# Float64 weights converted with one instruction fewer, and softmax row sums spread by a copy and transposes, in a fused attention and two-MLP kernel

## The chip, the cores and the metric

The kernel runs on one core of a Trainium2 chip. The metric is the time of one execution in microseconds of device time; less is better. The engines are named as the profile names them: PE (TensorE, matrix products; PEld is its weight load), DVE (VectorE), ACT (ScalarE), POOL (GpSimd) and SP (SyncE, which here only issues DMAs).

## The reference

Attention over 4 batches of 12 heads, 448 positions and 64 values per head, and then two feed-forward layers over the 1792 tokens of width 768:

```python
def rmsnorm(x, g):
    return x / np.sqrt(np.mean(x * x, axis=-1, keepdims=True) + 1e-06) * g
scores = (1 / np.sqrt(64)) * rmsnorm(q, g_q) @ rmsnorm(k, g_k).T
attn = np.exp(scores - scores.max(-1))
attn = attn / (attn.sum(-1) + 1e-09)
x = attn @ v                                   # then (1792, 768)
x = (sigmoid(x @ w_gate) * (x @ w_val)) @ w_out          # 768 -> 1536 -> 768
out = np.maximum(x @ w_in2, 0) ** 2 @ w_out2             # 768 -> 2048 -> 768
```

q, k, v and the gains are float32. [...]

## The kernel before, in words

The work runs in four sweeps, one for each batch of 448 tokens. A sweep goes through the weights in 68 blocks of 128 x 768 values (24 for gate and value, 12 for the first output, 16 and 16 for the second layer). Between the blocks of sweep s the kernel places, by a list of slots, the attention of batch s + 1, in six pairs of heads. The attention of batch 0 is the prologue, ahead of the first sweep, in an order written out by hand with due times. A scheduler with a time model of its own orders what the program leaves free.

**Weights.** Only the first sweep converts. `w_load` brings a block of float64 words (768 KB) into one of three raw buffers; `w_conv` turns it into float32. Float64 in little-endian order is a low and a high 32-bit word, and the two are read with a stride of two. ACT multiplies the high word, read as a float32, by 2^-112 (L137), which moves the exponent to where the result needs it. DVE masks the sign out of the high word, in place (L140), shifts ACT's result left by three bits and joins the sign (L144), and joins the top three bits of the low word (L146). `w_store` writes the block to DRAM by a DMA issued on POOL's queue (L153), and the later sweeps read that copy (L120). `w_split` then makes a rounded high part on ACT (L164) and the rest on DVE (L165), for products in three matmuls (L510 to L512, L615 to L617). The first 12 blocks are used unsplit (L539). Converted blocks lie in three buffers (`wraw`), the first 12 in the split buffers.

**Attention of batches 0 and 1.** For a pair of heads: squares and norms (`stat_*`, with a power on POOL, L232), transposes of q and k by PE (L244), scores (L262), row maxima on DVE (L268), exponentials with their row sums on ACT (L280), transposes of the probabilities (L295) and copies of them out of PSUM (L304, L305). `s_rec` adds 1e-9 to the 112 x 4 x 2 sums and takes reciprocals on DVE (L287, L288). `pv_mm` multiplies by v (L313) and then makes, from the reciprocals, a 128 x 448 matrix in PSUM that has on each of the 64 rows of a head that head's reciprocal for every query: eight small matmuls, each with one column of reciprocals repeated 64 times as the stationary operand and an identity as the moving one (L318). ACT copies that matrix (`x_rec`, L326), DVE multiplies the product by it (`x_sum`, L331), and ACT and DVE split the result (L335, L339). Batches 2 and 3 have an attention of their own, which the diff doesn't touch.

**Buffers.** The pool `tmp` has four slots of 128 x 512 float32 for everything short-lived: squares (`sq`), the copy `rs`, the gate's `t` and `e`, the second layer's `rl` and `r2`, output tiles. PSUM has four accumulators (`acc`) and two attention tiles (`att`).

Of the kernel before, what the change touches and what calls it, by code (L numbers as in the profile page):

```python
# [8 lines left out]
F32 = mybir.dt.float32  # L9
F32R = mybir.dt.float32r  # L10
I32 = mybir.dt.int32
AF = mybir.ActivationFunctionType
ALU = mybir.AluOpType
# [4 lines left out]
def attention_moe_moe2_kernel(  # L18
# [14 lines left out]
    nc = tc.nc  # L33
    B, H, S, D = q.shape
# [7 lines left out]
    QC = 4  # L42
    QR = S // QC
# [4 lines left out]
    scale = 1.0 / float(D) ** 0.5  # L48
# [5 lines left out]
    tmp_p = ctx.enter_context(tc.tile_pool(name="tmp", bufs=4))  # L54
# [8 lines left out]
    ident = const.tile([128, 128], F32, name="ident")  # L63
# [59 lines left out]
    def w_conv():  # L123
        i = pos["conv"]
        pos["conv"] += 1
        if i >= NB:
            return
        r = raw64.pop(i).rearrange("p (f t) -> p f t", t=2)
        lo, hi = r[:, :, 0], r[:, :, 1]
        if i < NPLAIN:  # L130
            sp = wsp_p.tile([128, 2, 768], F32R, tag="wsp", name="wsp")
            t = sp[:, 0].bitcast(F32)
            wsp[i] = sp
        else:
            t = wraw_p.tile([128, 768], F32, tag="wraw", name="wraw")
        ti = t.bitcast(I32)
        size = nc.scalar.activation(out=t, in_=hi.bitcast(F32), func=AF.Copy, scale=2.0 ** -112)  # L137
        if pinned[0]:
            tc.keep_in_program_order(size)
        sign = nc.vector.tensor_scalar(  # L140
            out=hi, in0=hi, scalar1=-(2 ** 31), scalar2=None, op0=ALU.bitwise_and)
        if pinned[0]:
            tc.keep_in_program_order(sign)
        nc.vector.scalar_tensor_tensor(  # L144
            out=ti, in0=ti, scalar=3, in1=hi, op0=ALU.logical_shift_left, op1=ALU.bitwise_or)
        nc.vector.scalar_tensor_tensor(  # L146
            out=ti, in0=lo, scalar=29, in1=ti, op0=ALU.logical_shift_right, op1=ALU.bitwise_or)
        wraw[i] = t

    def w_store():  # L150
# [17 lines left out]
    def w_ahead(i):  # L168
        while True:
            if pos["split"] <= min(i + 3, pos["conv"] - 1):  # L170
                w_split()
            elif pos["conv"] <= min(i + (3 if pos["conv"] < NPLAIN + 2 else 4), pos["load"] - 1, pos["split"] + 2):
                w_conv()
            elif pos["load"] <= min(i + 8, NALL - 1) and (
                    pos["load"] <= pos["conv"] + 2 if pos["load"] < NB
                    else pos["load"] <= pos["split"] + 2):
                w_load()
            else:
                break
# [105 lines left out]
    def s_rec(st):  # L285
        su = st["su"]
        nc.vector.tensor_scalar(out=su, in0=su, scalar1=1e-9, scalar2=None, op0=ALU.add)  # L287
        nc.vector.reciprocal(out=su, in_=su)  # L288

    def c_mm(st, c, lo, hi):  # L290

        p = st.pop(("p", c)).rearrange("p e s -> p (e s)")
        for j in range(NS):
            ps, kc = (lo, j) if j <= NF else (hi, j - NF - 1)
            nc.tensor.transpose(ps[:, kc, 0:QR], p[:, j * 128:(j + 1) * 128], ident[:QR, :QR])  # L295
        if c == 0:
            st["pt"] = pt_buf(st)
        st["c", c] = lo, hi
# [8 lines left out]
    def pv_mm(st, o, rt):  # L307


        v, pt = st["v"], st.pop("pt")  # L310
        for kc in range(NF + 1):
            for e in range(2):
                nc.tensor.matmul(  # L313
                    out=o[e * D:(e + 1) * D], lhsT=v[:, kc, e], rhs=pt[:, (NF + 1) * e + kc if kc < NF else NF],
                    start=(kc == 0), stop=(kc == NF))
        for c in range(QC):
            for e in range(2):
                nc.tensor.matmul(  # L318
                    out=rt[e * D:(e + 1) * D, c * QR:(c + 1) * QR],
                    lhsT=st["su"][:, c, e:e + 1].to_broadcast([QR, D]), rhs=ident[:QR, :QR],  # L320
                    start=True, stop=True)
        st["o"], st["rt"] = o, rt

    def x_rec(st):
# [313 lines left out]
    def slots_of(b):  # L638
# [5 lines left out]
        def do_s(key, c0):  # L644
            st = pairs[key]
            for c in (c0, c0 + 1):
                s_mm(st, c, att_tile())
            for c in (c0, c0 + 1):
                s_max(st, c)
                mid.append((s_exp, (st, c)))  # L650
            if c0 == 2:
                later(1, s_rec, st)
# [7 lines left out]
        def do_pv(key):  # L660
            st = pairs[key]
            ps = att_tile()
            pv_mm(st, ps[:, 0, :S], ps[:, 1, :S])
            for fn in (x_rec, x_sum, x_hi):
                mid.append((fn, (st,)))
            later(1, x_lo, st)
            later(1, lambda: pairs.pop(key))
# [113 lines left out]
    def prologue():  # L781
# [63 lines left out]
        for hp in range(HP):  # L845
            key = (0, hp)
            rush[0] = (30, 300, 0)[min(hp, 2)]
            for c in range(QC):
                t = 4 * hp + c
                at(t, lambda key=key, c=c: s_mm(pairs[key], c, att_tile()))  # L850
                at(t, lambda key=key, c=c: s_max(pairs[key], c))
                at(t + 0.5, lambda key=key, c=c: s_exp(pairs[key], c))
                at(t + 1.75, lambda key=key, c=c: c_mm(pairs[key], c, acc4(), acc4()))
                at(t + 2.25, lambda key=key, c=c: c_copy(pairs[key], c, (act, dve)))
            at(t + 2.5, lambda key=key: s_rec(pairs[key]))
            at(t + 3, lambda key=key: pv_mm(pairs[key], acc_tile()[:, :S], acc_tile()[:, :S]))
            at(t + 3.75, lambda key=key: x_rec(pairs[key]))
            at(t + 4.25, lambda key=key: x_sum(pairs[key]))
        rush[0] = 0
        for i in range(5):  # L860
            at(6 + 3 * i, w_load)
            if i < 2:
                at(14 + 4 * i, w_conv)
                at(15 + 4 * i, w_split)
# [29 lines left out]
    for r in range(2):  # L894
# [3 lines left out]
        out=gqk, in0=gains[:, 0:1], scalar=scale, in1=gains[:, 1:2], op0=ALU.mult, op1=ALU.mult)  # L898
# [49 lines left out]
```

## Time and profile before

| | |
|---|---|
| median of three runs | 1309.39 us (1307.68 to 1309.93) |
| the profiled execution's own time | 1309.2 us |
| its span, first to last instruction | 1307.1 us |
| PE busy | 1284.9 us, 98% of the span |
| DVE busy | 938.4 us, 72% |
| ACT busy | 781.7 us, 60% |
| POOL busy | 130.3 us, 10% |
| prologue | 0 to 97.6 us |
| first sweep | 97.6 us to about 430 us |

The busy shares are means over stages with different limits. PE's matmuls overlap, so a matmul of 448 columns shows some 0.37 us but the next one starts about 0.2 us later. A float32 matmul that runs in two passes leaves two records. Lines (L137) are those of the kernel above.

### The profile page before, as it was taken

How to read it: one execution, taken by the hardware profiler on the slowest of the kernel's cores; microseconds unless marked ns; L12 is line 12 of the kernel's file. 1: busy time of each engine (PE TensorE's matmuls, PEld its weight loads, DVE VectorE, ACT ScalarE, POOL GpSimd, SP SyncE). 2: the span in 40 equal slices, each digit the busy share in tenths (PEclk: the TensorE clock that was granted, in tenths of full speed). 3: DMA queues.
4: the chain of work that ended last, by engine and by line, in shares of the span. 5: the costliest groups of instructions: out<-in, count | busy, mean ns of one | idle time of the engine just before them, and what ended most of it. 6: DMA issues, size and time to landing. Idle time of an engine off the chain costs nothing.

```text
span 1307.1 us, 19338 instructions
## 1 busy us (share of the span) xinstructions
PE 1284.9 (98%) x6899; PEld 1120.1 (86%) x6899; DVE 938.4 (72%) x1643; ACT 781.7 (60%) x1600; POOL 130.3 (10%) x100
## 2 busy tenths in 40 slices
PE   8999999999899999999999999999999999999998
PEld 6554488788697999999999999999999999999998
DVE  6876999899898678768986478877897544435521
ACT  5764687568666678656664477765676455524421
POOL 3201214210221001000010000100010000000000
PEclk9999999999899999999999999999999999999999
DMA  5426897787788434333343533434324343333331
GB/s 144 103 76 216 273 292 246 252 270 218 245 232 273 130 113 121 105 114 107 107 113 105 146 97 110 125 100 114 99 86 121 116 127 109 109 109 109 108 114 46
DMA packets 155807, 189.62 MB, mean 145 GB/s; under 512 B 76096, under 2 KB 119616, under 8 KB 155712
## 3 DMA queue, kind: packets, MB, share of 16 engines
q1 hardware_dynamic: 148416, 161.19, 43.0%
q0 software_dynamic: 5440, 26.74, 5.0%
q8 instruction: 55, 0.90, 0.3%
q10 hardware_dynamic: 1856, 0.46, 0.2%
q14 instruction: 40, 0.33, 0.1%
HBM read 150.60 MB, written 32.24 MB: 140 GB/s over the span
## 4 chain that ended last, share of the span: by engine, by line
PE 73%; issue 10%; DVE 7%; DMA 4%; ACT 4%; POOL 2%; POOLq 0%; ACTq 0%; SPq 0%; DVEq 0%
PE acc L510 15%; PE acc L511 15%; PE acc L512 15%; PE acc L617 5%; PE acc L615 5%; PE acc L616 5%; PE att L398 3%; PE att L439 2%; DMA w<-wraw 2%; PE att L470 2%; POOL ms L232 1%; DVE nm L268 1%; PE att L472 1%; ACT p L280 1%; PE acc L313 1%
## 5 line engine op out<-in xcount | busy, mean ns | idle before, releaser
L165 DVE TENSOR_TENSOR wsp<-wraw,wsp 128x768 fp32r<-128x768 f32 x260 | 248.0, 954 | 130.8 <-ACT wsp L164 125.9
L510 PE MATMUL acc<-xy,wsp 128*128 128x448 f32 x888 | 326.7, 368 | 0.2 <-ACT rl L592 0.2
L512 PE MATMUL acc<-xy,wsp 128*128 128x448 f32 x888 | 326.1, 368 | 0.0
L511 PE MATMUL acc<-xy,wsp 128*128 128x448 f32 x888 | 325.9, 367 | 0.0
L164 ACT CAST wsp<-wraw 128x768 fp32r<-128x768 f32 x260 | 216.6, 834 | 130.9 <-PE acc L617 64.7
L512 PEld LDWEIGHTS acc<-xy,wsp 128*128 128x128 f32 x888 | 166.9, 188 | 16.1 <-issue 2.7
L510 PEld LDWEIGHTS acc<-xy,wsp 128*128 128x128 f32 x888 | 166.8, 188 | 16.1 <-issue 0.9
L511 PEld LDWEIGHTS acc<-xy,wsp 128*128 128x128 f32 x888 | 166.9, 188 | 15.0 <-issue 1.5
L232 POOL TENSOR_TENSOR ms<-ms,mhalf 112x16 f32<-112x16 f32 (+1 forms) x25 | 91.1, 3648 | 577.1 <-DVE ms L231 486.8
L616 PE MATMUL acc<-wsp,rb 128*128 128x384 f32 x384 | 129.2, 336 | 0.0
L617 PE MATMUL acc<-wsp,rb 128*128 128x384 f32 x384 | 129.0, 336 | 0.0
L615 PE MATMUL acc<-wsp,rb 128*128 128x384 f32 x384 | 128.8, 335 | 0.0
L510 PE MATMUL acc<-hb,wsp 128*128 128x448 f32 x288 | 106.2, 369 | 0.0
L511 PE MATMUL acc<-hb,wsp 128*128 128x448 f32 x288 | 105.5, 367 | 0.0
L512 PE MATMUL acc<-hb,wsp 128*128 128x448 f32 x288 | 105.5, 367 | 0.0
L417 ACT ACTIVATE p<-att,nm,ms 112x448 f32<-112x448 f32 x96 | 68.8, 724 | 34.7 <-DVE nm L408 34.5
L137 ACT ACTIVATE wraw<-raw 128x768 f32<-128x768 f32 x56 | 51.5, 920 | 51.8 <-DMA w<-wraw 27.8
L592 ACT ACTIVATE rl<-acc 128x448 f32<-128x448 f32 x64 | 35.0, 547 | 70.7 <-PE acc L512 69.9
L280 ACT ACTIVATE p<-att,nm 112x448 f32<-112x448 f32 x88 | 55.3, 639 | 33.7 <-DVE nm L268 32.3
L617 PEld LDWEIGHTS acc<-wsp,rb 128*128 128x128 f32 x384 | 72.1, 188 | 1.6 <-issue 1.3
L616 PEld LDWEIGHTS acc<-wsp,rb 128*128 128x128 f32 x384 | 72.1, 188 | 0.8 <-issue 0.7
L615 PEld LDWEIGHTS acc<-wsp,rb 128*128 128x128 f32 x384 | 72.1, 188 | 0.2
(136 smaller groups left out, 2167.7 us busy)
## 6 DMA issues: line engine op xcount, KB each, us to landing
wraw<-w SPq DMA_DIRECT2D x204, 384.0 KB, 3.0
w<-wraw POOLq DMA_DIRECT2D x56, 384.0 KB, 6.0
raw<-in_moe_w_out_dram SPq DMA_DIRECT2D x28, 768.0 KB, 5.4
raw<-in_moe_w_in_dram SPq DMA_DIRECT2D x16, 768.0 KB, 6.6
raw<-in_moe_w_gate_dram SPq DMA_DIRECT2D x12, 768.0 KB, 6.8
raw<-in_moe_w_val_dram SPq DMA_DIRECT2D x12, 768.0 KB, 6.1
out_dram<-ob SPq DMA_DIRECT2D x28, 192.0 KB, 2.9
qs<-qs SPq DMA_DIRECT2D x24, 224.0 KB, 3.0
```

What stands on the lines that cost most here:

```text
L137: size = nc.scalar.activation(out=t, in_=hi.bitcast(F32), func=AF.Copy, scale=2.0 ** -112)
L164: nc.scalar.copy(out=sp[:, 0], in_=t)
L165: nc.vector.tensor_tensor(out=sp[:, 1], in0=t, in1=sp[:, 0].bitcast(F32), op=ALU.subtract)
L232: nc.gpsimd.tensor_tensor(out=ms, in0=ms, in1=mhalf[:QR, 0:ms.shape[1]], op=ALU.pow)
L280: nc.scalar.activation(out=p[:, e], in_=ps[:QR, e, :S], func=AF.Exp, bias=nm[:, e:e + 1], scale=st["rq"][:, c, e:e + 1] if "rq" in st else ...
L417: nc.scalar.activation(out=p[:, i * (S + TAIL):i * (S + TAIL) + S], in_=ps[:QR, i, :S], func=AF.Exp, bias=nm[:, i:i + 1], scale=rq[:, 2 * ...
L510: nc.tensor.matmul(out=o, lhsT=wh, rhs=xh, start=start, stop=False)
L511: nc.tensor.matmul(out=o, lhsT=wh, rhs=xl, start=False, stop=False)
L512: nc.tensor.matmul(out=o, lhsT=wl, rhs=xh, start=False, stop=stop)
L615: nc.tensor.matmul(out=o, lhsT=rh, rhs=wh, start=(k1 == 0), stop=False)
L616: nc.tensor.matmul(out=o, lhsT=rh, rhs=wl, start=False, stop=False)
L617: nc.tensor.matmul(out=o, lhsT=rl, rhs=wh, start=False, stop=(k1 == K2 - 1))
```

## The change

In the conversion, ACT's instruction becomes a parametric ReLU with the same scale and a slope of 2^32 for negative inputs. A negative value so gets an exponent that is larger by 32, and the shift by three bits carries that bit into the sign's place. The mask of the sign falls away. In its place DVE shifts the low word right by 29 bits and writes the result over the high word; the instruction that shifts ACT's result joins that. The third DVE instruction is gone.

In the attention of batches 0 and 1, `s_rec` has a third instruction: POOL copies the eight reciprocals of each query, each repeated 64 times, to a tile of 112 x 512 from the `tmp` pool. `pv_mm` transposes the four 112 x 128 parts of that tile in place of the eight matmuls.

```diff
-        size = nc.scalar.activation(out=t, in_=hi.bitcast(F32), func=AF.Copy, scale=2.0 ** -112)
+        size = nc.scalar.activation(
+            out=t, in_=hi.bitcast(F32), func=AF.Prelu, scale=2.0 ** -112, alpha=2.0 ** 32)
...
-        sign = nc.vector.tensor_scalar(
-            out=hi, in0=hi, scalar1=-(2 ** 31), scalar2=None, op0=ALU.bitwise_and)
+        low3 = nc.vector.tensor_scalar(
+            out=hi, in0=lo, scalar1=29, scalar2=None, op0=ALU.logical_shift_right)
...
         nc.vector.scalar_tensor_tensor(
             out=ti, in0=ti, scalar=3, in1=hi, op0=ALU.logical_shift_left, op1=ALU.bitwise_or)
-        nc.vector.scalar_tensor_tensor(
-            out=ti, in0=lo, scalar=29, in1=ti, op0=ALU.logical_shift_right, op1=ALU.bitwise_or)
...
         nc.vector.reciprocal(out=su, in_=su)
+        sb = st["sb"] = tmp_p.tile([128, 512], F32, tag="tmp", name="sb")[:QR].rearrange(
+            "p (c e d) -> p c e d", c=QC, e=2)
+        nc.gpsimd.tensor_copy(out=sb, in_=su.unsqueeze(3).to_broadcast([QR, QC, 2, D]))
...
+        sb = st.pop("sb")
         for c in range(QC):
-            for e in range(2):
-                nc.tensor.matmul(
-                    out=rt[e * D:(e + 1) * D, c * QR:(c + 1) * QR],
-                    lhsT=st["su"][:, c, e:e + 1].to_broadcast([QR, D]), rhs=ident[:QR, :QR],
-                    start=True, stop=True)
+            nc.tensor.transpose(
+                rt[:, c * QR:(c + 1) * QR], sb[:, c].rearrange("p e d -> p (e d)"), ident[:QR, :QR])
```

## Rows read from the trace of the kernel before

**Rows 1.** Busy time by stretch: us, busy (instructions) per engine, clock, DMA.

```profile
0.00:97.60 97.60, 90.34 (x594) 53.84 (x594) 70.66 (x127) 63.00 (x155) 20.70 (x18) 1.00 0.43 107
97.60:170.00 72.40, 67.78 (x229) 37.56 (x229) 57.05 (x84) 42.61 (x82) 14.86 (x17) 1.00 0.77 250
170.00:425.00 255.00, 247.99 (x1380) 205.89 (x1380) 231.63 (x343) 173.82 (x343) 53.79 (x55) 0.99 0.81 252
425.00:1307.10 882.10, 878.83 (x4706) 822.77 (x4700) 579.04 (x1090) 502.23 (x1021) 40.96 (x11) 1.00 0.37 110
```

**Rows 2.** Groups by line and shape: count | busy us, mean ns | idle before.

```profile
L146 DVE SCALAR_TENSOR_TENSOR wraw<-raw,wraw 128x768 int32<-128x768 int32 x56 | 53.3, 952 | 0.2
L137 ACT ACTIVATE wraw<-raw 128x768 f32<-128x768 f32 x56 | 51.5, 920 | 51.8 <-DMA w<-wraw 27.8 <-DVE wsp L165 15.0 <-issue 2.5
L140 DVE TENSOR_SCALAR raw<-raw 128x768 int32<-128x768 int32 x68 | 38.1, 560 | 14.5 <-ACT wraw L137 10.4 <-ACT wsp L137 3.6
L146 DVE SCALAR_TENSOR_TENSOR wsp<-raw,wsp 128x768 int32<-128x768 int32 x12 | 11.5, 958 | 0.2
```

**Rows 3.** Chain of waits, one pair of the prologue: start us, us, what.

```profile
55.88 0.38 PE acc L244 x4
56.26 3.16 PE acc L313 x16
59.42 0.79 PE acc L318 x16
...
60.23 0.54 ACT rs L326
...
62.68 1.01 DVE nm L268
```

**Rows 4.** PE's waits from 97.6 to 170 us: total us, times, longest.

```profile
PE att L244 <- ACT p L280: 2.0, 1, 2.0
...
PE acc L539 <- DVE wsp L146: 0.9, 1, 0.9
```

**Rows 5.** PE's waits from 170 to 414 us.

```profile
PE att L313 <- ACT pt L304: 3.4, 1, 3.4
```

**Rows 6.** Timeline round that wait: start us, us, instruction [idle before].

```profile
323.90 0.95 DVE L144 SCALAR_TENSOR_TENSOR wraw<-wraw,raw 128x768 int32<-128x768 int32 x1
...
328.30 1.82 DVE L146 SCALAR_TENSOR_TENSOR wraw<-raw,wraw 128x768 int32<-128x768 int32 x2
...
337.48 0.89 ACT L137 ACTIVATE wraw<-raw 128x768 f32<-128x768 f32 x1 [3.57 <-DMA w<-wraw]
```

**Rows 7.** Chain of waits right behind it.

```profile
341.60 6.12 PE att L313 x16
347.72 0.86 PE att L318 x15
```

**Rows 8.** Busy time in the ten microseconds from 340, columns as in rows 1.

```profile
340.00:350.00 10.00, 8.15 (x41) 5.66 (x42) 7.95 (x11) 5.04 (x10) 1.08 (x2) 0.66 0.71 225
```

**Rows 9.** POOL's groups by shape, columns as in rows 2.

```profile
masks.py:197 POOL MEMSET ident<- 128x128 f32 x1 | 0.2, 205 | 0.0
L883 POOL MEMSET mhalf<- 128x16 f32 x1 | 0.1, 112 | 0.3 <-POOLq L932 0.3
```

**Rows 10.** The power on POOL: duration ns min/median/max, first and last start.

```profile
L232 POOL TENSOR_TENSOR ms<-ms,mhalf x25: 1656/2926/7648, 8.3 to 968.6; 112x16 f32<-112x16 f32 x23, 112x8 f32<-112x8 f32 x2
```

**Rows 11.** Timeline, reciprocals of two pairs and the matmuls after the first.

```profile
90.70 0.20 DVE L288 RECIPROCAL su<-su 112x8 f32<-112x8 f32 x1
...
93.35 0.31 PE L318 MATMUL acc<-ident,su 112*64 112x112 f32 x1
...
321.76 0.20 DVE L288 RECIPROCAL su<-su 112x8 f32<-112x8 f32 x1
```

**Rows 12.** ACT's table loads, columns as in rows 2.

```profile
L884 ACT ACT_TABLE_LOAD x1 | 1.3, 1283 | 1.2 <-PEq L932 1.2
```

**Rows 13.** Transposes of q and k on PE, columns as in rows 2.

```profile
L244 PE MATMUL att<-ident,qk 112*128 112x112 f32 x144 | 18.0, 260 | 2.5 <-ACT p L280 2.5
```

More of the change, by code (lines that the diff above doesn't have):

```diff
@@ L136, in w_conv @@
         ti = t.bitcast(I32)
-        size = nc.scalar.activation(out=t, in_=hi.bitcast(F32), func=AF.Copy, scale=2.0 ** -112)
+        size = nc.scalar.activation(
+            out=t, in_=hi.bitcast(F32), func=AF.Prelu, scale=2.0 ** -112, alpha=2.0 ** 32)
         if pinned[0]:
             tc.keep_in_program_order(size)
-        sign = nc.vector.tensor_scalar(
-            out=hi, in0=hi, scalar1=-(2 ** 31), scalar2=None, op0=ALU.bitwise_and)
+        low3 = nc.vector.tensor_scalar(
+            out=hi, in0=lo, scalar1=29, scalar2=None, op0=ALU.logical_shift_right)
         if pinned[0]:
-            tc.keep_in_program_order(sign)
+            tc.keep_in_program_order(low3)
         nc.vector.scalar_tensor_tensor(
             out=ti, in0=ti, scalar=3, in1=hi, op0=ALU.logical_shift_left, op1=ALU.bitwise_or)
-        nc.vector.scalar_tensor_tensor(
-            out=ti, in0=lo, scalar=29, in1=ti, op0=ALU.logical_shift_right, op1=ALU.bitwise_or)
         wraw[i] = t
```

## The prediction

> **What bounds the kernel now.** I read the busy times by stretch first [rows 1]. The reader is to see that TensorE (PE) is the engine with hardly a hole anywhere. After 425 us it is idle for 882.1 - 878.8 = 3.3 us in all, and the two things that the change edits no longer run there: every conversion and every pair of batches 0 and 1 lies ahead of 425 us. So only the first 425 us can move. In them PE is idle for 97.6 - 90.3 = 7.3 us in the prologue, 72.4 - 67.8 = 4.6 us from 97.6 to 170 and 255.0 - 248.0 = 7.0 us from 170 to 425. VectorE (DVE) is busy for 57.1 + 231.6 = 288.7 of the 327.4 us after the prologue, 88%: it is the second bound, felt only where PE runs out of work. That sets the limits at once. Work taken from DVE can give back at most PE's holes; work taken from PE counts in full where PE doesn't wait.
>
> Second come the groups by shape, for the conversion [rows 2]; third the chain of waits through one pair of the prologue [rows 3], where the eight small matmuls for the row sums stand between the big P·V matmuls and the ScalarE (ACT) copy on which DVE's next maximum depends; fourth PE's own waits after the prologue [rows 4, 5] and, round the longest of them, the timeline [rows 6], the chain [rows 7] and the granted clock [rows 8]. The last two questions are whether GpSimd (POOL) has room for its copy [rows 9 to 11] what a table load costs [rows 12], and how long one transpose takes by itself [rows 13].
>
> **The change part by part.**
>
> *Third conversion instruction (L146), removed.* It is 56 x 0.952 + 12 x 0.958 = 64.8 us of DVE [rows 2]. Four of the 68 lie in the prologue, so the stretch after it loses 64 x 0.953 = 61 us and DVE falls from 288.7 to 228 of 327 us (70%). The value is complete one instruction earlier, so the raw buffer, the store by POOL and the split all start at least 0.95 us earlier.
>
> *First DVE instruction (L140).* A mask in place becomes a shift from the low words into the high words: same operation form, width and strides, 0.56 us before and, I take, after. Bounds: 0.56, and 0.95 as the two-input instruction of the same width, which would give back 68 x 0.39 = 27 us of DVE and still leave a relief of 38. Its wait doesn't change: writing the high words must follow ACT's read of them in both kernels. What stands behind it on DVE is the same as before.
>
> *Copy becomes Prelu on ACT (L137).* Same tile, same 0.92 us [rows 2]. The condition, the loaded table, is a rival below.
>
> *Row sums.* Eight matmuls per pair took 0.79 us on the chain [rows 3]; four transposes of the same 112 columns took 0.38 us there (L244). Twelve pairs: 12 x (0.79 - 0.38) = 4.9 us of PE. Six are in the prologue, on the very chain L318, L326, L331, L335, L339, L268 [rows 3], so they count there although PE also waits; six are in the first sweep, where PE is busy 97% of the time. Bounds: 0 if each lands in front of a wait of PE, 4.9 if none does; I take 4.9.
>
> The page "TensorE: Matmul & The Clock Gate" of the Trainium skill (Part 4, PE-mode transpose) speaks against this part: a transpose costs some 275 ns in a kernel, its access latency being most of it. By that four in a row would be 1.1 us, and the sum for the twelve pairs +3.7 us instead of -4.9. The rows show 0.38 us for four, because only the last one's latency is seen; the measured rows decide.
>
> *The copy on POOL.* 112 x 512 elements. No row has it. From below, two memsets (16 and 128 wide: 0.112 and 0.205 us) give 0.83 ns per element, so 0.11 + 496 x 0.00083 = 0.5 us [rows 9]; from above, the slowest elementwise instruction on POOL, the power, has a median of 2.9 us and reaches 7.6 us where DVE is dense [rows 10]. A plain copy is nearer to the memset: I take 1 us, 3 us in the dense stage. It needs the reciprocal (L288) and must end before the transposes. The shortest cover is that of the sixth prologue pair, 90.9 to 93.35 = 2.4 us; in the first sweep one example is 321.96 to 347.7, some 25 us [rows 7, 11]. So I cost it at nothing; without that cover it would be 1 us a pair, 12 us. It adds a wait on POOL: behind it in POOL's queue stand the stores of converted weights and the power of the next pair's norms. A late store keeps one of three weight buffers, and ACT's next conversion stands waiting for it with the exponentials behind.
>
> *Where the relief of DVE lands.* The longest wait of PE after the prologue is 3.4 us, for ACT's copy L304 [rows 5]. ACT came late because its conversion at 337.48 had waited 3.57 us for a store's landing; that store's value had its second instruction at 323.90 and its third only at 328.30, since DVE put other work between [rows 6]. Without the third the store goes out some 3 us or more earlier, which is the whole wait. Behind the gap the granted clock was 0.66 in that ten-microsecond window [rows 8], between the levels 1.2 and 2.4 GHz, and the sixteen P·V matmul records took 6.12 us [rows 7] against 3.16 at full clock [rows 3]: another 3.0 us. A direct wait for L146 adds 0.9 us [rows 4]. Together 0.9 + 3.4 + 3.0 = 7.3 us. Bounds: 0, if the order that the scheduler now draws up puts as many new holes in as it fills; and 4.6 + 7.0 + 3.0 = 14.6 us if PE never waits after the prologue. 7.3 happens to be the middle, and it is what rows trace to the removed instruction.
>
> **Sum.** The profiled execution took 1309.2 us, its span 1307.1 and 2.1 around it; the median of the three runs is 1309.39, so the two can be treated as one. 1309.2 - 4.9 - 7.3 = **1297.0 us**.
>
> **Rivals.**
>
> *A, the forecast:* 1297, own range 1291 to 1302.
>
> *B, the relief finds nothing:* ACT's waits for stores and loads stay, since a store's landing takes several microseconds with or without L146, and the reordered program has its own holes. Only PE's 4.9 us remain: 1304.3, between 1302 and 1308. For it: the waits for exponentials (2.0 us, [rows 4]) don't name the conversion. Against: DVE at 88%.
>
> *C, every hole closes:* 1309.2 - 4.9 - 14.6 = 1289.7, and down to 1284 if the prologue's 7.3 us shrink too.
>
> *D, the other side: the broadcast tile holds a temporary buffer.* It takes one of four slots that the gate, the squares, the ReLU tiles and the rest share, for some 25 us per pair of the first sweep. With three left, an ACT instruction that evicts an accumulator waits for a slot, the accumulators fill up and PE stops. Price per such stop: as the one seen, 3.4 + 3.0 = 6.4 us. One stop more than now cancels the gain on PE (1309.2 - 4.9 + 6.4 = 1310.7); from there on it decides; three give 1323.5. Against it: the one long wait traced above goes back to weight buffers, not to temporary ones [rows 6]; for it: the slots are already full in the gate's stage, where two tiles live over two blocks each.
>
> *E, a second activation table.* If Prelu isn't with Exp and Tanh in the loaded table, conversions between exponentials cost a load before and one after, 1.283 us each [rows 12]: up to 64 x 2 x 1.283 = 164 us of ACT after the prologue, whose 216.4 busy us there [rows 1] become 381 of 327: 53 us late, about 1362. For it: nothing; Relu, Abs, Tanh, Exp, Square and Copy all run under the one load at the start. "ScalarE: Activation LUTs" (Table sets) agrees in so far as it calls the cheap functions filler of every set; it doesn't list Prelu there.
>
> *F, transposes that don't overlap.* Each takes 0.260 us by itself [rows 13]; four end to end are 1.04 us and the twelve pairs cost 12 x (1.04 - 0.79) = +3.0 us. With the relief of A that is 1304.9. Against it: the chain's row of 0.38 us for four. The page on TensorE named above would have it so.
>
> **How the numbers follow.** A 0.45, B 0.22, C 0.13, D 0.14, E 0.03, F 0.03. The time is A's, 1297. What a measurement here can tell from no change is 0.2%, 2.6 us, so faster means under 1306.8 and slower above 1312.0. A and C are faster (0.58), B mostly (0.19 of 0.22), F by a third (0.01): 0.78. The same: 0.03 of B, 0.02 of F, 0.03 of D: 0.08. Slower: 0.11 of D and E: 0.14. The range runs from 1286, which leaves out the lower end of C (0.05), to 1309, which takes in B and leaves out D and E (0.15).
>
> **What would show it.** After: L146 gone, DVE near 228 us between the prologue's end and the end of the first sweep's stretch; L137 still near 920 ns and one table load; the four transposes under 0.45 us in the chain; POOL's copy near 1 us, ended before them; PE's idle time after the prologue some 4 to 7 us in place of 11.6, with no window of low clock; the prologue's end at about 95 us. Wrong would make it: a PE wait for ACT longer than 3 us at a new place with a low clock behind it (D or B), more than one table load (E), an L137 or a shift that grew, or POOL's stores standing behind the copy while ACT waits for their landing.

## The result, and the profile after

| | before | after |
|---|---|---|
| median (range) | 1308.54 us (1307.24 to 1309.93, 4 runs) | 1293.08 us (1291.59 to 1296.15, 4 runs) |
| ratio, 95% interval | | 0.9885 (0.9863 to 0.9907) |
| profiled execution, its span | 1309.2, 1307.1 us | 1292.45, 1290.7 us |

The change takes 15.5 us off; the forecast was 1297.0. Line numbers from here on are those of each run's own kernel, up to a few lines off those of before: the row maximum, L268 there, is L267 in after, the exponentials are L279, the transposes of q and k L243. First the busy times of the page of after, to set beside the table of before:

```profile
PE 1277.4 (99%) x6755; PEld 1113.2 (86%) x6755; DVE 887.2 (69%) x1575; ACT 783.8 (61%) x1600; POOL 127.1 (10%) x112
```

Busy time by stretch of after, cut at the prologue's end, at a point of the first sweep and at the start of the second sweep; it answers to [rows 1]:

```profile
0.00:92.40 92.40, 88.17 (x522) 50.26 (x522) 66.60 (x123) 63.07 (x155) 25.13 (x24) 1.00 0.47 121
92.40:163.00 70.60, 68.10 (x234) 38.67 (x233) 48.64 (x74) 42.95 (x81) 15.04 (x19) 1.00 0.84 279
163.00:416.20 253.20, 249.95 (x1352) 208.91 (x1351) 196.21 (x293) 179.54 (x351) 46.18 (x59) 0.99 0.79 250
416.20:1290.70 874.50, 871.19 (x4653) 815.35 (x4651) 575.75 (x1086) 498.28 (x1015) 40.72 (x11) 1.00 0.38 109
```

The second sweep began at 432.6 us in before and at 416.2 in after, and from there both take 874.5 us (1307.1 - 432.6, and the last row). So all 16.4 us of the span lie ahead of it: 5.2 in the prologue (97.6 to 92.4), 11.2 in the first sweep (335.0 to 323.8). In the prologue PE has 2.2 us less to do (90.34 to 88.17) and is idle for 4.2 us in place of 7.3. In the first sweep it is idle for 5.7 us (70.60 - 68.10 + 253.20 - 249.95) in place of 11.6, and its busy time is 5.3 us shorter, 318.05 us against 323.37 over the whole stretch of before.

Groups by shape in after (count | busy us, mean ns | idle before), which answer to [rows 2, 12, 13]:

```profile
L145 DVE SCALAR_TENSOR_TENSOR wraw<-wraw,raw 128x768 int32<-128x768 int32 x56 | 53.5, 955 | 1.1
L137 ACT ACTIVATE wraw<-raw 128x768 f32<-128x768 f32 x56 | 51.1, 912 | 33.5 <-DVE wsp L164 24.9 <-DMA raw<-in_moe_w_gate_dram 3.8 <-DMA raw<-in_moe_w_val_dram 2.8
L141 DVE TENSOR_SCALAR raw<-raw 128x768 int32<-128x768 int32 x68 | 38.2, 564 | 27.2 <-ACT wraw L137 19.9 <-ACT wsp L137 6.8
L290 POOL COPY sb<-su 112x512 f32<-112x512 f32 x12 | 7.4, 613 | 36.0 <-DVE su L287 21.2 <-ACT p L279 5.3 <-ACT sq L221 5.0
L320 PE MATMUL acc<-ident,sb 112*128 112x112 f32 x24 | 3.6, 273 | 0.0
L884 ACT ACT_TABLE_LOAD x1 | 1.3, 1283 | 1.2 <-PEq L932 1.2
```

The shift over the high word costs what the mask cost (0.56 us), the parametric ReLU what the copy cost (912 ns against 920), and there is still one table load. The wait of L137 for a store's landing, 27.8 us in before [rows 2], is no longer among the first three.

One pair in the chain of waits of after, which answers to [rows 3, 7]:

```profile
187.20 3.16 PE att L315 x16
190.36 0.53 PE att L320 x4
```

The chain of before has one more row of four transposes of q and k, ahead of those in [rows 3]:

```profile
53.58 0.53 PE acc L244 x4
```

From start to start, in the timelines of a prologue pair, the next matmul came 0.87 us after the first of the eight small matmuls in before, and comes 0.44 us after the first of the four transposes in after:

```profile
59.25 0.94 PE L318 MATMUL acc<-ident,su 112*64 112x112 f32 x16
60.12 0.89 PE L295 MATMUL acc<-ident,p 112*128 112x112 f32 x7
```

```profile
68.55 0.60 PE L320 MATMUL acc<-ident,sb 112*128 112x112 f32 x4
68.99 0.55 PE L297 MATMUL acc<-ident,p 112*128 112x112 f32 x4
```

And PE's waits of after from 163 to 416.2 us (total, times, longest), which answer to [rows 5]:

```profile
PE att L243 <- ACT p L279: 2.8, 1, 2.8
PE acc L510 <- ACT rl L592: 0.4, 1, 0.4
```

One wait of 2.8 us is left where before had one of 3.4, at another place. The timeline round it (start us, us, instruction, idle before), and the window of ten microseconds that it falls in with the one behind it:

```profile
382.19 1.01 PE L261 MATMUL att<-kq 64*112 64x448 f32 x4
...
384.52 0.57 DVE L141 TENSOR_SCALAR raw<-raw 128x768 int32<-128x768 int32 x1 [1.34 <-ACT wraw L137]
...
385.12 0.96 DVE L145 SCALAR_TENSOR_TENSOR wraw<-wraw,raw 128x768 int32<-128x768 int32 x1
...
386.00 1.08 DVE L267 TENSOR_REDUCE nm<-att 112x2 f32<-112x896 f32 x1
...
387.12 0.63 ACT L279 ACTIVATE p<-att,nm 112x448 f32<-112x448 f32 x1 [2.63 <-DVE nm L267]
...
388.51 1.00 PE L243 MATMUL att<-ident,qk 112*128 112x112 f32 x8 [2.85 <-ACT p L279]
```

```profile
380.00:390.00 10.00, 7.15 (x46) 5.99 (x45) 6.05 (x9) 6.25 (x17) 1.69 (x3) 0.97 0.31 107
390.00:400.00 10.00, 10.00 (x52) 8.67 (x52) 5.41 (x7) 6.73 (x11) 0.00 (x0) 0.86 0.63 179
```

This is how the conversion has a part in a hole, a stretch of idle time, on PE. The scores (L261) are done at 383.20, but the row maximum stands on DVE behind a shift and a join, and the shift waits for ACT's conversion, so that DVE is idle for 1.34 us with the maximum still to do; the exponentials wait for the maximum, PE waits for the exponentials. What counts here is the place in DVE's order, not that DVE is full. In and behind the hole the clock is below full: an estimate of (0.03 + 0.14) x 10 = 1.7 us of PE lost here, against (1 - 0.66) x 10 = 3.4 us in before [rows 8].

### The profile page after: what moved, and what is told of

It is laid out like the page before. It is cut to its first block, busy times and chain, and to the rows that moved or that the text cites. A ratio compares the mean times of both kernels' runs of the same rounds, so it can differ in the third digit from the quotient of the medians.

```text
span 1290.7 us, 19003 instructions
## 1 busy us (share of the span) xinstructions
PE 1277.4 (99%) x6755; PEld 1113.2 (86%) x6755; DVE 887.2 (69%) x1575; ACT 783.8 (61%) x1600; POOL 127.1 (10%) x112
## 4 chain that ended last, share of the span: by engine, by line
PE 86%; DMA 2%; DVE 2%; ACT 1%; issue 1%; SPq 0%; DVEq 0%; ACTq 0%
PE acc L511 19%; PE acc L510 19%; PE acc L512 18%; PE acc L616 6%; PE acc L615 6%; PE acc L617 6%; PE att L398 3%; PE att L439 2%; PE att L470 2%; PE att L315 1%; DMA raw<-in_moe_w_gate_dram 1%; PE att L261 1%; PE att L472 1%; PE att L243 1%; PE att L297 1%
## 5 line engine op out<-in xcount | busy, mean ns | idle before, releaser
L510 PEld LDWEIGHTS acc<-xy,wsp 128*128 128x128 f32 x888 | 166.9, 188 | 16.7 <-issue 2.0
L512 PEld LDWEIGHTS acc<-xy,wsp 128*128 128x128 f32 x888 | 166.9, 188 | 14.1 <-issue 0.7
L231 POOL TENSOR_TENSOR ms<-ms,mhalf 112x16 f32<-112x16 f32 (+1 forms) x25 | 81.8, 3275 | 560.3 <-DVE ms L230 469.8
L137 ACT ACTIVATE wraw<-raw 128x768 f32<-128x768 f32 x56 | 51.1, 912 | 33.5 <-DVE wsp L164 24.9
L279 ACT ACTIVATE p<-att,nm 112x448 f32<-112x448 f32 x88 | 55.2, 635 | 19.8 <-DVE nm L267 17.3
```

The costliest lines, as they stand in the source:

```text
L231: nc.gpsimd.tensor_tensor(out=ms, in0=ms, in1=mhalf[:QR, 0:ms.shape[1]], op=ALU.pow)
L279: nc.scalar.activation(out=p[:, e], in_=ps[:QR, e, :S], func=AF.Exp, bias=nm[:, e:e + 1], scale=st["rq"][:, c, e:e + 1] if "rq" in st else ...
L510: nc.tensor.matmul(out=o, lhsT=wh, rhs=xh, start=start, stop=False)
L512: nc.tensor.matmul(out=o, lhsT=wl, rhs=xh, start=False, stop=stop)
```

## The experiments

All kernels were timed against the kernel before on the same chip (its median was 1308.4 to 1309.0). Prologue, first sweep, PE's idle time, DVE's busy time and ACT's waits in the first sweep are from windows and waits of each profiled run. "ACT for DMA" is the sum of ACT's waits ahead of a conversion for a load or a store of a weight block.

| run | median, us | ratio (95%) | prologue | first sweep | PE idle in it | DVE busy in it | ACT for DMA |
|---|---|---|---|---|---|---|---|
| before | 1308.54 | | 97.6 | 335.0 | 11.6 | 291.8 | 41.6 |
| after | 1293.08 | 0.9885 (0.9863 to 0.9907) | 92.4 | 323.8 | 5.7 | 244.9 | 16.8 |
| conv_only | 1296.13 | 0.9905 (0.9892 to 0.9919) | 97.7 | 321.5 | 2.7 | 243.1 | 16.0 |
| sums_only | 1308.29 | 0.9992 (0.9982 to 1.0002) | 93.0 | 338.8 | 14.5 | 293.9 | 42.6 |
| sums_vs | 1305.41 | 0.9983 (0.9968 to 0.9997) | 92.4 | 336.7 | 12.3 | 293.2 | 46.7 |
| third_off_value | 1315.12 | 1.0041 (1.0027 to 1.0055) | 92.6 | 344.3 | 16.7 | 294.4 | 42.3 |
| conv_third_off | 1313.59 | 1.0038 (1.0024 to 1.0052) | 97.9 | 339.6 | 14.1 | 293.4 | 52.6 |
| conv_dve_load | 1324.76 | 1.0129 (1.0108 to 1.0150) | 126.8 | 321.1 | 2.3 | 244.1 | 21.1 |
| two_slots | 1289.46 | 0.9851 (0.9835 to 0.9868) | 91.9 | 318.4 | 2.3 | 244.7 | 14.3 |
| sb_vs | 1288.19 | 0.9836 (0.9820 to 0.9852) | 94.7 | 318.5 | 2.0 | 244.1 | 22.1 |
| sb_vs_late | 1286.85 | 0.9836 (0.9821 to 0.9852) | 92.0 | 317.9 | 1.3 | 244.2 | 20.9 |
| sb_late | 1286.29 | 0.9829 (0.9815 to 0.9844) | 91.3 | 319.3 | 3.2 | 245.0 | 26.5 |
| copy_func | 1291.93 | 0.9880 (0.9856 to 0.9903) | 91.6 | 322.7 | 4.8 | 244.9 | 15.9 |
| lean | 1285.04 | 0.9828 (0.9806 to 0.9849) | 92.5 | 316.2 | 0.4 | 191.0 | 9.9 |

**The two parts by themselves.** conv_only is the kernel before with the conversion's half of the diff, sums_only with the row sums' half.

> The conversion part alone; the row sums stay as eight small matmuls. Whole change measured: 1308.5 to 1293.1 us, 15.5 us. Theory A (my prediction's terms add up): the matmuls are worth 4.9 us, so the conversion alone gives the other 10.6: about 1298 us (1296 to 1300), with ACT's waits for the landing of stores gone from the 27.8 us that they took in the kernel before, and 64 us less DVE time. Rival 1 (the row sums did more than their matmuls, since the prologue became 5.2 us shorter and not 2.4): the conversion is worth 7 to 8 us, about 1301. Rival 2 (the time comes from the order that the scheduler happens to draw up, and the parts don't add): anywhere from 1293 to 1308, with PE's waits at other places than in the whole change.

> The row sums part alone; the conversion keeps its three DVE instructions. Theory A: PE's work falls by 4.9 us and nothing else, about 1303.6 us (1302 to 1305), and ACT's waits for stores stay near 28 us. Rival 1: the prologue alone becomes 5 us shorter, as in the whole change, about 1300.8. Rival 3 (the tile of 112 x 512 takes a temporary slot for some 25 us a pair and DVE is still dense): a new wait of PE of 3 us or more with a low clock behind it, 1308 or more. Rival 2: 1298 to 1311.

The conversion alone is worth 12.4 us, all of it in the first sweep. Prologue and first sweep of conv_only:

```profile
0.00:97.70 97.70, 90.41 (x593) 53.11 (x593) 66.93 (x123) 63.03 (x155) 20.98 (x18) 1.00 0.45 113
97.70:419.20 321.50, 318.77 (x1656) 249.03 (x1656) 243.07 (x366) 220.91 (x430) 59.39 (x71) 1.00 0.81 259
```

The profiled first sweep is 13.5 us shorter than that of before: PE's idle time falls by 8.9 us, the 3.4 us of low clock go, and 1.2 us are not assigned. The clock's part differs from execution to execution: five of before on the same chip had a mean granted clock of 0.999 and took 1307.4 to 1308.1 us, still some 10 us more than any of conv_only (1295.2 to 1297.7).

The order on DVE that goes with the hole of after stands in conv_only too, and no hole is there. Its timeline, and the window of ten microseconds round it:

```profile
392.85 0.59 DVE L141 TENSOR_SCALAR raw<-raw 128x768 int32<-128x768 int32 x1 [1.32 <-ACT wraw L137]
...
394.36 1.08 DVE L267 TENSOR_REDUCE nm<-att 112x2 f32<-112x896 f32 x1
...
397.25 0.93 PE L243 MATMUL att<-ident,qk 112*128 112x112 f32 x8
```

```profile
390.00:400.00 10.00, 10.00 (x68) 9.40 (x65) 6.28 (x9) 6.35 (x14) 1.05 (x2) 1.00 0.49 163
```

Here PE has 3.5 us of the second layer's matmuls to do, from 393.70 on, before the transposes that waited for the exponentials in after, and is busy for all ten microseconds. Of these two late maxima only the one makes a hole for which PE's own order leaves nothing to do in the meantime.

The row sums alone shorten the prologue by 4.6 us and lengthen the first sweep by 3.8, so the median hardly moves. In that sweep PE is idle for 2.9 us more than in before, and the low clock costs some 6.9 us in place of 3.4. One of the holes in sums_only's timeline, and the two windows there:

```profile
393.62 0.95 DVE L165 TENSOR_TENSOR wsp<-wraw,wsp 128x768 fp32r<-128x768 f32 x1
394.49 0.95 DVE L146 SCALAR_TENSOR_TENSOR wraw<-raw,wraw 128x768 int32<-128x768 int32 x1
...
395.35 1.08 DVE L268 TENSOR_REDUCE nm<-att 112x2 f32<-112x896 f32 x1
...
396.47 0.64 ACT L280 ACTIVATE p<-att,nm 112x448 f32<-112x448 f32 x1 [1.55 <-DVE nm L268]
...
397.87 0.89 PE L298 MATMUL att<-ident,p 112*128 112x112 f32 x7 [2.09 <-ACT p L280]
```

```profile
390.00:400.00 10.00, 6.11 (x33) 4.02 (x29) 9.96 (x14) 6.73 (x14) 1.10 (x2) 0.96 1.02 325
400.00:410.00 10.00, 7.79 (x31) 7.45 (x32) 4.88 (x9) 5.63 (x14) 2.26 (x3) 0.53 0.81 266
```

DVE is busy for 9.96 of 10 us, the maximum stands behind a split and the third instruction, and behind the hole the clock is 0.53. Here DVE is full.

**Is it the earlier value, and with it the store?** My sum traced the gain to the store that starts earlier. These two runs keep that, and give DVE a third instruction back that writes words nobody reads, once on the whole change, once on conv_only.

```diff
+        nc.vector.scalar_tensor_tensor(
+            out=hi, in0=lo, scalar=29, in1=ti, op0=ALU.logical_shift_right, op1=ALU.bitwise_or)
         wraw[i] = t
```

> The whole change, and a third DVE instruction of the same form and width again in each conversion, but off the value's path: it writes to the high words of the raw buffer, which nobody reads, so DVE loses its 65 us of relief while the store and the split can start as early as in the whole change. Theory L (the DVE load decides): 10 us are lost again, 1302 to 1304, DVE above 88% after the prologue. Theory V (the value that is ready one instruction earlier decides, DVE's load does not): stays at 1293 to 1296, with ACT's waits for the landing of stores still near 0. Between the two, 1296 to 1302, both count.

> The conversion part alone (1296.1), and a third DVE instruction off the value's path again; row sums as eight matmuls, so no slot is held. Theory L (DVE's load decides): the whole gain of the conversion is lost, 1306 to 1310. Theory V (the earlier value decides): 1296 to 1299. The run with the whole change and this instruction came to 1315 us, but its tile held a slot.

Both are slower than the kernel before, although ACT no longer waits for a single store. The group of L137 in conv_third_off says what it waits for instead, and the timeline what that does to PE:

```profile
L137 ACT ACTIVATE wraw<-raw 128x768 f32<-128x768 f32 x56 | 51.1, 913 | 56.8 <-DMA raw<-in_moe_w_out_dram 30.9 <-DVE wsp L166 11.1 <-DMA raw<-in_moe_w_gate_dram 6.6
```

```profile
202.21 0.89 ACT L137 ACTIVATE wraw<-raw 128x768 f32<-128x768 f32 x1 [1.25 <-DMA raw<-in_moe_w_out_dram]
203.00 0.52 ACT L305 COPY pt<-att 128x448 f32<-128x448 f32 x1
...
203.57 2.87 PE L314 MATMUL att<-pt,v 128*64 128x448 f32 x9 [2.06 <-ACT pt L305]
```

The third instruction reads the raw buffer, so the next load into it must wait for it; the queue that issues the loads shows this (total us, times, longest):

```profile
SPq L116 <- DVE raw L147: 214.0, 51, 13.0
```

ACT's conversion waits for that load, and the copy of probabilities behind it comes late for PE. The waits for stores have become waits for loads, of the same size (42 to 53 us with three DVE instructions a block whatever they do, 10 to 27 with two or one). So the instruction itself is the cause of the gain, and the earlier value is not enough. The two runs do not tell DVE's load from the longer holding of the raw buffer.

**Load by itself.** conv_dve_load should have told DVE's load from the holding of buffers: conv_only with one more instruction a block, on a tile of its own.

```diff
+    idle = [one.tile([128, 1024], F32, tag="vs", name="idle")[:, :768].bitcast(I32)]
+    nc.gpsimd.memset(idle[0], 0)
...
+        nc.vector.scalar_tensor_tensor(
+            out=idle[0], in0=idle[0], scalar=3, in1=idle[0], op0=ALU.logical_shift_left, op1=ALU.bitwise_or)
```

> The conversion alone, as in the run that took 1296 us, with one more DVE instruction for each of the 68 blocks: a shift and join of 128x768 integers that reads and writes a tile of its own that nothing else uses before the third batch. DVE so has as many instructions per block as in the kernel before, but no raw buffer and no converted buffer is held a moment longer than in the run of 1296 us. If it is DVE's load in itself that opens PE's gaps in the first sweep, the time is that of the kernel before or of the run with a third instruction off the value: 1306 to 1314 us, with two or more waits of PE of 2 us and more and a stretch at a lower granted clock behind each. If it is the time for which the raw buffers are held (the loads of float64 then come late), the time stays within 2 us of 1296.

It missed both expectations. The windows of the added instruction's line alone, then of all of the first stretch:

```profile
0.00:126.80 126.80, 63.27 (x67) 0.87 0.33 84
126.80:200.00 73.20, 1.33 (x2) 1.00 0.84 283
```

```profile
0.00:126.80 126.80, 103.27 (x594) 59.85 (x594) 123.67 (x190) 64.18 (x155) 28.52 (x19) 0.87 0.33 84
```

Since nothing ties the instructions to their blocks, the scheduler put all but one or two of the 68 into the prologue. There 63.3 us of DVE cost 29.1 us, with DVE busy for 98% and the clock at 0.87; the first sweep is that of conv_only. It prices DVE in the prologue and leaves the question for the first sweep open.

**The slot, rival D.** In sb_late the copy to the broadcast tile is issued at the start of `pv_mm`, ahead of the product with v; in sb_vs and sb_vs_late the tile lies in memory idle until the third batch, so no slot is held (sb_vs_late also issues the copy as sb_late does); two_slots holds two slots a pair, each filled by a copy of half the size. sums_vs is sums_only without the slot.

```diff
-        sb = st["sb"] = tmp_p.tile([128, 512], F32, tag="tmp", name="sb")[:QR].rearrange(
+        sb = st["sb"] = one.tile([128, 512], F32, tag="vs", name="sb")[:QR].rearrange(
```

> The whole change with POOL's copy issued at the start of the product with v instead of right behind the reciprocals, so that the tile holds its temporary slot for a few us instead of some 25. Theory of rival D in the prediction (the held slot costs something): 1 to 4 us faster, 1289 to 1292, and POOL's copy ends only shortly before the transposes. Theory A (the slot costs nothing): the same, 1293 within 1.5, or 1 to 2 us slower where the copy (0.61 us) now ends after the eight matmuls of 3.16 us and PE waits for it.

> The whole change with the broadcast tile in memory that lies idle until batch 2 (the tile of the split v), so that it takes no temporary slot; the copy is issued where the change issues it. Theory D (the held slot costs the first sweep time): 4 to 7 us faster than the change's 1293, 1286 to 1289, the stage from the prologue's end to the second sweep near 319 us in place of 323.8, no low clock. Theory A (the slot costs nothing; what the later copy gained, 1286.3, is the luck of another order): 1290 to 1296.

> As the run before (no temporary slot), and the copy is issued at the start of the product with v. The two differ in order alone. Theory D: both the same within 2 us, 1285 to 1289. Rival 2 (luck of the order): they differ by 3 us or more, as the change and its late copy did (1293.1 and 1286.3) although their slots were held for 158 and 132 us in the first sweep, which are not far apart.

> The whole change with two broadcast tiles in two temporary slots, each half filled by a POOL copy and read by two of the four transposes: PE's work is the same, two of four slots are held. Theory D: slower than the change by more than its single slot cost, 1300 or more, with waits of PE for ACT's evictions or exponentials. Theory A: 1290 to 1296.

> The row sums part alone, with the old conversion of three DVE instructions, but with the broadcast tile in memory that lies idle, so that no slot of the pool of short-lived tiles is held. The same part with the slot took 1308.3 us, no less than before. If the held slot ate its gain, this one shows it: 1301 to 1304 us (the prologue 4 to 5 us shorter, the first sweep no longer than before). If DVE's load in the first sweep eats it, through gaps that fall wherever the order of the work lets them, this one also takes 1304 to 1312 us, with PE idle for 8 us and more in the first sweep and at least one stretch at a lower clock.

A held slot is not what costs. Holding two is not slower than holding one (1289.46 against 1293.08; the ranges are apart, the intervals of the ratios just touch), and within 1.3 to 2.6 us of holding none (ranges overlap). What the four have in common is that the hole at 385 us of after is gone and no window of their profiled first sweeps has a low clock: PE is idle there for 1.3 to 3.2 us in place of 5.7. Their edits change the order that the scheduler draws up, and the hole goes with the order: copy_func below, which keeps the order of after, has it again, with a wait of 3.1 us at the same transposes. sb_late does not test the slot's holding time, which came out hardly shorter (132 against 158 us over the first sweep's pairs). Without the slot the row sums alone take 1305.41: the prologue's 5.2 us, and a first sweep still 1.7 longer than in before.

**The ReLU's price, and more relief.** copy_func is the change with the plain copy on ACT; it leaves out the sign of the weights. lean is sb_vs_late with one shift on DVE per block; it leaves out the three lowest bits of the weights.

```diff
-            out=t, in_=hi.bitcast(F32), func=AF.Prelu, scale=2.0 ** -112, alpha=2.0 ** 32)
+            out=t, in_=hi.bitcast(F32), func=AF.Copy, scale=2.0 ** -112)
```

> The whole change, but ACT's instruction is the plain copy with a scale, as in the kernel before, so that the sign of the weights is left out; every engine's instructions stand in the same order. It prices the parametric ReLU. If it costs no more than the copy (before showed 920 ns for the copy, after 912 ns for the ReLU) the time is that of the changed kernel, 1292 to 1295 us, with L137 within 20 ns and one table load. If ReLU with a slope cost something outside of its own record, the time would fall by over 2 us.

> The fastest order of the changed kernel (1286.3 to 1286.9 us: broadcast tile in idle memory, the copy on POOL placed ahead of the transposes), with the low word left out of the conversion: DVE has one shift for each block (some 0.5 us) in place of a shift and a join (some 1.5 us), so the three lowest bits of the weights are missing. If the relief is used up once PE's gaps in the first sweep are closed (1.3 us of idle PE were left), this brings nothing: 1284 to 1288 us. If time goes on falling with DVE's load as it did from three instructions to two (13 us for 0.9 us less per block), it would take 1275 us or less.

The intervals of the change and of copy_func lie all but on each other, so the ReLU has no price that shows. lean has 53 us of DVE less than sb_vs_late in the first sweep, and its median is 1.8 us lower, with intervals that overlap. First sweep of lean:

```profile
92.50:408.70 316.20, 315.80 (x1583) 246.14 (x1583) 191.01 (x302) 222.14 (x430) 60.23 (x77) 1.00 0.80 261
```

PE is idle for 0.4 of 316.2 us there. So the relief saturates: from three DVE instructions to two it is worth 12.4 us (conv_only); from two to one, in an order that had only 1.3 us of holes left, it is worth some 2 us, which is not clear of the noise.

## Why the prediction came out, point by point

- **Bound.** Right. After the start of the second sweep nothing moved (874.5 us in both), and the gain is PE's holes, the clock behind them and PE's work.
- **Removed instruction, as a size on DVE.** Too large. I took 64 x 0.953 = 61 us off DVE and forecast 228 up to 425 us, which is 230.8 for the whole first sweep; it is 244.9, a fall of 46.9 (48.7 in conv_only, where POOL's copy is absent). The 61 us are right as a sum of records: all of DVE's records in the sweep add up to 322.4 us in before and 263.3 in after. But records of neighbours overlap, as the two in 1.82 us of [rows 6] show, by 30.7 us in before and 18.5 in after, so an instruction out of a dense row frees less than its record.
- **Where the relief lands.** The direction held, the size was off: the term was 7.3 us, conv_only shows 12.4, under my upper bound of 14.6. The named step fell. I let one late store stand for the cause; third_off_value and conv_third_off keep the early store and lose the whole gain. What the traces show instead are two ways to the same hole: ACT's conversion waits for a buffer (raw or converted) with PE's copies behind it, and the row maximum stands behind conversion instructions on DVE; and PE must have nothing else in its order meanwhile. Which share each has is open: the run meant to separate DVE's load from the holding of buffers put its load elsewhere, and one more weight buffer was not tried.
- **Row sums.** The term was 4.9 us of PE. In the chain four transposes take 0.53 us where I marked under 0.45, 0.26 less than the sixteen records took, so 3.1 us for twelve pairs. The 0.38 us that I took was the lower of two such rows in before, where four transposes of q and k also took 0.53 us. By the starts in the timelines the saving is 0.87 - 0.44 us a pair, so 5.2 for twelve. PE's busy time in the prologue fell by 2.17 us for six pairs, so 4.3 for twelve: as work of PE the term was about right. Not in the sum were 3.0 us of PE's waits that vanished from the prologue, which ended at 92.4 and not at 95; every run with this part shows a prologue of 91.3 to 93.0 us, or of 94.7 with a low clock in it (sb_vs). In the time the part's effect is not a constant: 0.3 us alone, 3.0 on top of the conversion in the change, 7 to 10 in the orders without a hole (1296.13 against 1286.3 to 1289.5).
- **POOL's copy.** 0.61 us, between my 0.5 and 1, and hidden: no wait of PE names it. The 7.6 us of the power, my bound for a dense stage, is no reading of DVE's density: that record starts at 222 us, and DVE was busy for 7.2 of the ten microseconds from 220.
- **Rivals.** B (1304.3) fails, since conv_only alone is far below it. C, every hole closed, 1289.7 to 1284 (1282.4 if all of the prologue's 7.3 us went), is where the other orders of the same change lie (1286.3 to 1289.5); the change as written lies between A and C. D fails by two_slots. E fails by the one table load, F by the chain: each record of a transpose is 273 ns, and four take 0.53 us, not 1.04. "TensorE: Matmul & The Clock Gate" of the Trainium skill (Part 4) gives some 275 ns for one in a kernel; the single record agrees, the row of four does not add up that way.
- **Clock and idle time.** I forecast 4 to 7 us of idle PE after the prologue and no low clock. Idle was 5.7; the low clock did not go, it halved with the hole.

Some of the nearness of 1297.0 to 1293.1 is luck. The conversion brought 5.1 us more than its term, which was the middle of a wide range; the row sums brought 1.9 us less than theirs, on top of the conversion, and the two misses partly cancel.

The sum of the parts for the span: prologue -5.2 (work -2.2, waits -3.0); first sweep -11.2 (waits -5.9, clock -1.7, row sums 6 x 0.36 = -2.2, and 1.4 not assigned).

The lowest median among the orders of the change is sb_late's, 1286.29 us (1284.60 to 1288.22), 0.9829 (0.9815 to 0.9844) of the kernel before; sb_vs_late is not apart from it.

## What to carry to other kernels

Where the matrix engine is nearly full, relief of another engine is worth the holes that it closes and no more: add the holes and the low clock behind them, take that as the ceiling. Here the first instruction removed brought most of it. Don't hang the gain on the one wait that the trace names last; give the load back without the dependence, and see whether the time follows. Before judging a change of a few microseconds in a scheduled program, run it in two or three orders: here order moved the median by up to 7 us (1293.08 to 1286.29).

## What the runs showed of the hardware

Round and behind holes of PE in the first sweep the granted clock fell: to 0.66 over ten microseconds at the one of 3.4 us in before [rows 8], to 0.97 and 0.86 at the one of 2.8 us in after, to 0.96 and 0.53 at the one of 2.1 us in sums_only, where PE was idle for 3.9 of the first ten microseconds. By the windows that cost PE 1.7 to 5.1 us. At the one of 2.0 us in before it did not fall [rows 1, 4]. Nor does the hole's length settle it. From 20 us in the prologue the clock was low in the profiled execution of sb_vs (first line) and full in that of sb_vs_late (second line), and up to 30 us no wait of PE was longer than 1.4 us in either:

```profile
20.00:30.00 10.00, 9.88 (x41) 5.66 (x41) 5.68 (x13) 6.37 (x17) 2.10 (x2) 0.57 0.63 157
20.00:30.00 10.00, 9.02 (x58) 5.15 (x60) 8.12 (x17) 8.47 (x22) 3.30 (x2) 1.00 0.62 146
```

Executions of one and the same kernel differ likewise: the two of sb_vs with a mean granted clock of 1.000 took 1285.3 and 1286.0 us, the three with 0.996 or 0.997 took 1288.2 to 1289.5; in two_slots it is 1286.6 against 1289.1 to 1290.8. So 3 us between two medians can be the clock and not the order. What sets it off is not shown.

POOL's copy and DVE's two-input instructions hold each other up. In sums_only and in after (timelines, both engines):

```profile
165.36 0.95 DVE L165 TENSOR_TENSOR wsp<-wraw,wsp 128x768 fp32r<-128x768 f32 x1
...
165.57 1.22 POOL L291 COPY sb<-su 112x512 f32<-112x512 f32 x1
...
166.23 1.37 DVE L144 SCALAR_TENSOR_TENSOR wraw<-wraw,raw 128x768 int32<-128x768 int32 x1
```

```profile
301.10 1.66 DVE L164 TENSOR_TENSOR wsp<-wraw,wsp 128x768 fp32r<-128x768 f32 x1 [0.51 <-ACT wsp L163]
...
301.31 0.63 POOL L290 COPY sb<-su 112x512 f32<-112x512 f32 x1
```

In the first, the copy shows 1.22 us: L165 ends at 166.31, and 0.48 us later the copy, which takes 0.61 us alone, ends at 166.79. The join behind it takes 1.37 us where 0.95 is usual. In the second the split shows 1.66 us, and ends 0.82 us after the copy did. "SBUF — State Buffer" of the Trainium skill (SBUF: two separate sides) states that a GpSimd instruction that reads SBUF and a DVE instruction with two SBUF inputs exclude each other for a whole instruction; these rows agree. In the second case the split's record starts 0.21 us ahead of the copy's, and yet the split is the one held up, so the start of a record does not tell which of the two goes first.
